# A branch turned round: the soft experts' stage as the fall-through arm

## The chip, the cores and the metric

One core of a Trainium2 chip. The metric is the device time of one execution in microseconds (us); the median of three runs of the kernel before is 814.7 us.

## The reference

Attention whose queries are averaged in pairs, then a layer that sends each of 2304 tokens to one of 8 experts, then a layer of 32 soft slots (4 for each of 8 experts). All arrays are float32.

```python
attn = softmax(scale * mean_of_2(q) @ k.T) @ v       # 4 x 8 heads, 1152 keys, 64 wide
x = attn.reshape(2304, 512)
e = argmax(x @ w_gate + bias); x = gate * relu(x @ w1[e]) @ w2[e]
logits = x @ phi                                     # 2304 x 32
slot_in  = softmax(logits, over tokens).T @ x        # 32 x 512
slot_out = relu(slot_in @ m2w1[e]) @ m2w2[e]         # 4 slots for each e
out = softmax(logits, over slots) @ slot_out         # 2304 x 512
```

## The kernel before

It has three stages: attention (to about 520 us), the experts (`ffn`, to about 760 us), the soft experts (`soft_moe`, to the end). All is written out in order by hand (`manual_schedule`): each engine works through its instructions in the order in which the program text issues them, and the framework adds semaphore waits.

The experts work on tasks of 256 tokens of one expert. The routing decides at run time how many there are. Eight (`NSTAT`) are written out; `g["n"]` holds the real count, which every engine reads into a register (L1660). Only if it is over 8 does `more` (L1662) run a loop of further tasks, the rare tasks: `with tc.If(g["n"] > NSTAT)` at L1666, with no other arm. With these inputs it is not over 8, so each engine's branch at L1666 jumps past the rare tasks' instructions. The rare block borrows the last four weight tiles as working room and loads them again at its end (L1669, four transfers by SP). A single matmul on the first weight tile (`NBR`, L1316) stands just ahead of the branch.

While tasks run, `Front.group` folds finished tokens into running sums: logits (L872, L876), a running maximum, `acc`, and the logits' transposed copy `lT`, which GpSimd scatters to DRAM (L918). The last group also makes the slot inputs `siT` (L850, L851).

`soft_moe` reads 32 weight tiles of 1 MB (`Stream`): 22 are fetched while the experts run, 10 as tiles come free. Its loop is paced by `step()` (L1455), once for each weight tile taken: it fetches, does what is in `todo`, and two entries of the list `soft` from the twelfth step on. At the first step SP loads all logits as `L` (L1459). `soft` normalises `L` over the slots and then, for each of five groups q of up to four token blocks, does two things. `c4(q)` is one copy on VectorE (L1386) of four blocks of `L` into `Cr`, a tile of which there is one (`CRB = 1`). `cT(q)` is four transposes of `Cr` on TensorE (L1392), a copy of the result to `cs` on ScalarE (L1394) and two subtractions on VectorE (L1396). Both halves of the expert layer are TensorE work on the weight tiles (L1472, L1486). The output is made in column parts (L1439), copied to `ob` (L1441) and stored by SP (L1443). `so` shares the place of `Cr`.

Of the kernel before, what the change touches and what calls it, by code (L numbers as in the profile page):

```python
# [24 lines left out]
DM = H * D  # L25
# [40 lines left out]
NWB = 0  # L66
NWR = (1, 1, 4)
RAWS = (1, 3)
CRB = 1
NBR = 1  # L70
WARM = 0
FILL = (0, 0, 2, 0, 0, 0, 2, 2, 2, 2)
# [720 lines left out]
class Front:  # L793
# [61 lines left out]
    def group(self, last=False):  # L855

        nc, g, xp = self.tc.nc, self.g, self.xp
        V = nc.vector
        bs, self.blocks = self.blocks, []
        n4 = len(bs)  # L860
        m = n4 * 32
        lanes = lambda c: slice(c * 32, (c + 1) * 32)
        small = lambda name: xp.tile([128, 128], F32, name=name, bufs=1)
        bank = lambda name: g["ps"].tile([128, 512], F32, name=name, tag="mx", bufs=3)
        d = {}

        def logits():
            lt = bank("lt")[:, 0:128]
            for c in range(n4):
                h, row = bs[c]["h"], bs[c]["row"]  # L870
                hot = g["ident"][:, row:row + 1] if isinstance(row, int) else row
                nc.tensor.matmul(lt[lanes(c)], hot.to_broadcast([128, NSL]), g["neg"][:, h * 128:(h + 1) * 128],  # L872
                                 start=True, stop=False)
            for k in range(4):
                for c in range(n4):
                    nc.tensor.matmul(lt[lanes(c)], g["phis"][:, k], bs[c]["yT"][:, k], start=False, stop=(k == 3))  # L876
            d["ls"], d["ex"] = small("ls"), small("ex")
            d["al"], d["se"], new = (xp.tile([128, 1], F32, name=x, bufs=2) for x in ("al", "se", "new"))
            d["al"], d["se"], nm = d["al"][:m], d["se"][:m], new[:m]
            V.reduce_max(d["se"], lt[:m], axis=AX.X)  # L880
            V.tensor_scalar(out=nm, in0=d["se"], scalar1=-1.0, scalar2=g["nm"][:m], op0=ALU.mult, op1=ALU.min)
            nc.scalar.activation(d["ex"][:m], lt[:m], AF.Exp, bias=nm)
            d["lt"] = lt
            nc.scalar.activation(d["al"], g["nm"][:m], AF.Exp, bias=nm, scale=-1.0)
            if m < 128:
                V.tensor_copy(g["nm"][:m], nm)
            else:
                g["nm"] = new

        def keep():  # L890
            V.tensor_copy(d["ls"][:m], d["lt"][:m])

        def flip():
            ep = bank("ep")
            d["eT"] = small("eT")
            nc.tensor.transpose(ep[:, :m], d["ex"][:m], g["ident"][:m, :m])
            nc.scalar.copy(d["eT"][:, :m], ep[:, :m])

        def turn_logits():
            lp = bank("lp")  # L900
            d["lT"] = g["lT"]
            nc.tensor.transpose(lp[:, :m], d["ls"][:m], g["ident"][:m, :m])
            V.tensor_copy(d["lT"][:, :m], lp[:, :m])

        def add():
            V.reduce_sum(d["se"], d["ex"][:m], axis=AX.X)
            V.scalar_tensor_tensor(out=g["sums"][:m], in0=g["sums"][:m], scalar=d["al"], in1=d["se"], op0=ALU.mult, op1=ALU.add)

        def rows():
            sin = bank("sin")  # L910
            for c in range(n4):
                nc.tensor.matmul(sin[lanes(c)], d["eT"][:, lanes(c)], bs[c]["y"], start=True, stop=True)
            V.scalar_tensor_tensor(out=g["acc"][:m], in0=g["acc"][:m], scalar=d["al"], in1=sin[:m], op0=ALU.mult, op1=ALU.add)

        def store(cs):
            done = []
            for c in cs:
                wr = nc.gpsimd.indirect_dma_start(out=g["ls"], out_offset=bass.IndirectOffsetOnAxis(ap=bs[c]["idx"], axis=0),  # L918
                                                  in_=d["lT"][:, lanes(c)], in_offset=None)
                for w in done:  # L920
                    self.tc.declare_no_dep(wr.ins, w.ins, reason="the rows are distinct")
                done.append(wr)
                if c != cs[-1]:
                    nc.gpsimd.memset(g["nop"], 0.0)


        twice = [c for c in range(n4) if bs[c]["row"] is AROW]
        rest = [c for c in range(n4) if c not in twice]
        first, late = (lambda: store(twice or rest)), (lambda: store(rest) if twice else None)
        if not last:  # L930
            return [None, logits, keep, None, flip, turn_logits, add, first, None, rows, None, late]
        common, weights, spread, total, slots = self.combine()
        return [None, logits, None, common, keep, None, flip, None, turn_logits, None, weights, None, add, spread, first, rows, None, total, None, slots]


# [103 lines left out]
def ffn(ctx, tc, g):  # L1039
# [214 lines left out]
    open_more(NWR[len(RAWS)])  # L1254
    flush(FILL)

    def more(room):

        own = room[1][:, 1024:2048]
        tio, pio, cnt = own[:, 0:MAXT], own[:, 16:17], own[:, 17:18]  # L1260
# [1 line left out]
            nc.gpsimd.iota(o, pattern=pat, base=0, channel_multiplier=cm, allow_small_or_imprecise_dtypes=True)  # L1262
        nc.gpsimd.memset(cnt, float(NSTAT))
        with tc.For_i(NSTAT, g["n"], 1):
            task(room, own, tio, pio, cnt)

    def task(room, own, tio, pio, cnt):

        V = nc.vector
        hot, on, tmp = own[:, 18:19], own[:, 32:32 + MAXT], own[:, 64:64 + 4 * MAXT].rearrange("p (q t) -> p q t", q=4)  # L1270
# [36 lines left out]
                nc.tensor.matmul(yp[h], ht[:, f, h * 128:(h + 1) * 128], wr[f // 2 % 2][:, c:c + DM], start=(f == 0), stop=(f == KF - 1))  # L1307
        todo.extend(front.put(yp, s["gt"], [xidx[:, h:h + 1] for h in range(2)], hot))
        todo.extend(front.group(True))
        flush()  # L1310


    warm = ps.tile([128, 512], F32, name="warm", tag="mx", bufs=3)
    first = g["ws"].tiles["m2w1", 0][0]
    for _ in range(NBR):
        nc.tensor.matmul(warm, g["ones128"], first[:, 0:512], start=True, stop=True)  # L1316
    g["more"](more)


class Stream:  # L1320


    def __init__(self, tc, g):
        self.tc, self.g = tc, g
        self.keys = [(w, i) for w in ("m2w1", "m2w2") for i in range(16)]
        self.tiles = {}
        self.free = []
        self.next = 0

    def add(self, pool, n):  # L1330
        self.free += [pool] * n

    def fetch(self, eng=None):
        if self.next < len(self.keys) and self.free:
            key = self.keys[self.next]
            pool = self.free.pop(0)
            tl = pool.tile([128, 2048], F32, name="mw")
            (eng or self.tc.nc.sync).dma_start(out=tl, in_=self.g[key[0]][key[1]])
            self.tiles[key] = (tl, pool)
            self.next += 1  # L1340
            return True
        return False

    def take(self, *key):
        tl, pool = self.tiles.pop(key)
        self.free.append(pool)
        return tl


def warm_up(nc, g, o, n):  # L1350
# [4 lines left out]
def soft_moe(ctx, tc, g):  # L1355
# [4 lines left out]
    V = nc.vector  # L1360
    cp = ctx.enter_context(tc.tile_pool(name="s_cp", bufs=1))
    siT = g["siT"]
    L = cp.tile([128, NI, NSL], F32, name="L")
    T3 = [128, NI, NSL]
    NR = (NI + 3) // 4
    if NWB:
# [15 lines left out]

    def c4(q):
        n4 = min(4, NI - 4 * q)
        Cr[q] = cp.tile([128, 4, 4, NSL], F32, name="Cr", tag="Cr", bufs=CRB)
        V.tensor_copy(Cr[q][:, :n4], L[:, 4 * q:4 * q + n4].unsqueeze(2).to_broadcast([128, n4, 4, NSL]))  # L1386

    def cT(q):
# [18 lines left out]
        lambda: c4(0),  # L1407
    ]
    for q in range(NR):
        if q + 1 < NR:  # L1410
            soft.append(lambda q=q: c4(q + 1))
        soft.append(lambda q=q: cT(q))

    def relu(r, hp):
        hs = cp.tile([128, 2, 512], F32, name="hs")
# [11 lines left out]
    def out_steps(h):  # L1427
# [5 lines left out]

        def some(i, c, i0, n4, ob):
            if i == i0:
                ob[0] = g["wa"].tile([128, 2048 // dw, dw], F32, name="ob", tag="mw")
            fo = bank("hp", 4).rearrange("p (c d) -> p c d", c=n)
            for k in range(c):
                nc.tensor.matmul(fo[:, k], cs[:, i + k], SO[h], start=True, stop=True)  # L1439
# [34 lines left out]
        todo += relu(r, hp)  # L1474
    first = [2 * KF * d0 // 512 for d0, _ in PARTS]
    for h, (d0, dw) in enumerate(PARTS):
        so = cp.tile([128, 2, DM // 2], F32, name="so", tag="Cr", bufs=CRB)[:, :, :dw]
        na = 512 // dw
        for r in range(2):
            op = bank("op", 2)[:, 0:dw]  # L1480
# [32 lines left out]
def moe_kernel(tc, qT, kT, vT, wg, mod, mbias, w1, w2, phi, m2w1, m2w2, k0, q0, out):  # L1513
    nc = tc.nc
    with ExitStack() as ctx:
# [2 lines left out]
        gf = c4.enter_context(tc.tile_pool(name="gf", bufs=1))  # L1518
        ga = c3.enter_context(tc.tile_pool(name="ga", bufs=1, side="right"))
        keep = {**dict.fromkeys(("ident", "ones128", "si", "sel", "xidx", "axidx", "nop"), gp),  # L1520
                **dict.fromkeys(("widx", "xidx", "ntask", "C", "agt", "awidx", "neg", "acc", "sums", "nm", "lT", "m4", "nmc", "w", "siw", "rc"), gf)}
        dr = ctx.enter_context(tc.tile_pool(name="dr", bufs=1, space=DRAM))
        g = dict(qT=qT, kT=kT, vT=vT, wg=wg, w1=w1, w2=w2, phi=phi, m2w1=m2w1, m2w2=m2w2, k0=k0, q0=q0, out=out)
        g["xs"] = dr.tile([PAD + N, XW], F32, name="xs")
# [21 lines left out]
        T([TB, NTB, 4], "sm")  # L1546
        T([TB, NTB, E], "ex")
        T([128, NSL], "si")
        g["phis"] = gf.tile([128, DM // 128, NSL], F32, name="phis")
        T([128, N // TS + 1], "jts")  # L1550
        T([128, MAXT], "tio")
        T([128, E], "eio")
# [3 lines left out]
            T([128, 1], nm)  # L1556
        T([128, NSL], "i32")
        T([1, 1], "nop")
        T([128, TS], "neg")
        T([128, DM], "acc")  # L1560
        T([128, 1], "sums")
        T([128, 1], "nm")
        T([128, 128], "lT")
        T([1, 4, NSL], "m4")
        T([128, 1], "nmc")
        T([128, 1], "w")
# [92 lines left out]
        def load_count():  # L1659
            g["n"] = nc.values_load(g["ntask"][0:1, 0:1], min_val=N // TS - 1, max_val=MAXT)  # L1660

        def more(task):  # L1662
            keys = list(ws.tiles)[-4:]
            room = [ws.tiles[key][0] for key in keys]

            with tc.If(g["n"] > NSTAT):  # L1666
                task(room)
                for key, tl in zip(keys, room):
                    nc.sync.dma_start(out=tl, in_=g[key[0]][key[1]])  # L1669

        g["load_count"] = load_count
        g["more"] = more
        with tc.manual_schedule():
            make_identity(nc, ident)
            g["ws"] = ws = Stream(tc, g)
# [1 line left out]
            with ExitStack() as c2:  # L1677
# [13 lines left out]
                g["open"] = open_weights  # L1691
                with ExitStack() as c1:
                    ffn(c1, tc, g)
            c4.close()
            with ExitStack() as c1:
                soft_moe(c1, tc, g)


def _layout(inputs):
# [41 lines left out]
```

## Time and profile before

| what | value |
|---|---|
| median of three runs | 814.7 us (814.34 to 814.75) |
| the profiled execution | 816.65 us |
| its span in the trace | 814.9 us |
| TensorE, VectorE, ScalarE, GpSimd busy | 96%, 69%, 57%, 66% |
| TensorE's instructions | 5674 matmuls, 5674 weight loads |
| granted TensorE clock, mean | 0.996 |

PE is TensorE's matmuls, PEld its weight loads, DVE VectorE, ACT ScalarE, POOL GpSimd, SP SyncE. A q behind a name (PEldq, SPq) is the engine's instruction queue: branches, semaphore events, DMA issues. "issue" is time in which an engine waited for nothing that the profile shows.

### The profile page before, as it was taken

What the parts mean: (1) busy time and instruction counts of PE and PEld (TensorE: products, weight loads), DVE (VectorE), ACT (ScalarE), POOL (GpSimd) and SP (SyncE); (2) the same over time, 40 slices, a digit from 0 to 9 for tenths busy, and PEclk for the clock granted to TensorE, in tenths of its full rate; (3) what the DMA queues carried; (4) which work ended last, traced back from release to release, by engine and by line L of the source; (5) the groups of instructions that cost most, each with busy time, mean ns of one, the idle gap of its engine ahead of it and who ended that gap; (6) DMA issues with size and microseconds to landing.
All of it is one profiled execution on the core that took longest, in us unless ns stands there. A gap on an engine that the chain in (4) does not pass through costs nothing.

```text
span 814.9 us, 15864 instructions
## 1 busy us (share of the span) xinstructions
PE 782.9 (96%) x5674; PEld 595.9 (73%) x5674; DVE 565.8 (69%) x1171; ACT 461.2 (57%) x1096; POOL 541.8 (66%) x501
## 2 busy tenths in 40 slices
PE   5899999999999999999999999999999999999897
PEld 5677777766677776777666668788898689988356
DVE  7587777678777877877878785766666556664252
ACT  5456565666865658766556873455555545554133
POOL 6879899999888988879978963534635544450200
PEclk9999999999999999999999999999999999999999
DMA  9876558667655676755554120786787887767987
GB/s 323 232 208 157 156 146 221 158 172 178 148 158 149 149 199 168 176 136 151 127 141 140 52 80 12 223 291 237 274 279 264 261 287 260 272 208 260 341 364 233
DMA packets 57782, 162.80 MB, mean 200 GB/s; under 512 B 14443, under 2 KB 21915, under 8 KB 53595
## 3 DMA queue, kind: packets, MB, share of 16 engines
q1 hardware_dynamic: 41604, 98.05, 42.7%
q0 software_dynamic: 13648, 47.32, 17.4%
q10 hardware_dynamic: 2448, 16.39, 5.6%
q8 instruction: 46, 0.75, 0.4%
q14 instruction: 36, 0.29, 0.1%
HBM read 110.45 MB, written 10.89 MB: 149 GB/s over the span
## 4 chain that ended last, share of the span: by engine, by line
PE 82%; DVE 5%; ACT 4%; POOL 3%; issue 3%; DMA 2%; SPq 0%; ACTq 0%; POOLq 0%; DVEq 0%
PE pv L272 17%; PE sc L252 12%; PE sc L258 8%; PE mps L203 7%; PE hp L774 4%; PE hp L776 4%; PE hp L775 4%; PE yp L788 4%; PE yp L790 3%; PE yp L789 3%; PE sg L305 2%; PE hp L1472 2%; PE op L1486 2%; PE tp L332 2%; DVE mxp L205 1%
## 5 line engine op out<-in xcount | busy, mean ns | idle before, releaser
L285 POOL TENSOR_TENSOR acc<-acc,e 128x576 f32<-128x576 f32 x214 | 315.2, 1473 | 23.6 <-ACT e L262 10.1
L262 ACT ACTIVATE e<-sc 128x288 f32<-128x288 f32 x576 | 223.7, 410 | 138.8 <-PE sc L258 116.1
L205 DVE TENSOR_REDUCE mxp<-mps 128x1 f32<-128x384 f32 x432 | 220.5, 549 | 94.2 <-PE mps L203 86.4
L252 PE MATMUL sc<-QS,KS 128*128 128x288 f32 x576 | 186.0, 331 | 3.3 <-ACT e L262 3.1
L258 PE MATMUL sc<-QL,KH 69*128 69x288 f32 x576 | 170.0, 298 | 1.5 <-DVE QL L223 1.2
L272 PE MATMUL pv<-e,V 128*64 128x288 f32 x1152 | 161.8, 416 | 0.0
L252 PEld LDWEIGHTS sc<-QS,KS 128*128 128x128 f32 x576 | 109.2, 190 | 56.4 <-issue 27.1
L203 PE MATMUL mps<-KS,QS 128*128 128x384 f32 x384 | 134.9, 356 | 11.5 <-ACT QS L468 7.0
L744 POOL DMA_INDIRECT wraw<-in_w,widx x72 | 73.9, 1026 | 106.3 <-DVE wlo L766 82.7
L272 PEld LDWEIGHTS pv<-e,V 128*64 128x64 f32 x1152 | 74.4, 137 | 60.2 <-issue 22.2
L258 PEld LDWEIGHTS sc<-QL,KH 69*128 69x128 f32 x576 | 109.3, 190 | 2.0 <-DVE QL L223 1.4
L766 DVE TENSOR_TENSOR wlo<-wraw,whi 128x512 fp32r<-128x512 f32 x136 | 90.7, 689 | 27.1 <-ACT whi L765 22.8
L765 ACT CAST whi<-wraw 128x512 fp32r<-128x512 f32 x136 | 79.6, 619 | 18.2 <-DMA wraw<-in_w,widx 14.0
L203 PEld LDWEIGHTS mps<-KS,QS 128*128 128x128 f32 x384 | 74.4, 194 | 14.8 <-ACT QS L468 7.4
L774 PE MATMUL hp<-xh,whi 128*128 128x256 f32 x256 | 73.2, 286 | 0.0
L776 PE MATMUL hp<-xh,wlo 128*128 128x256 f32 x256 | 71.9, 281 | 1.0 <-issue 0.8
L775 PE MATMUL hp<-xl,whi 128*128 128x256 f32 x256 | 71.8, 280 | 0.3 <-DVE xl L761 0.3
L283 POOL TENSOR_TENSOR acc<-e 128x576 f32<-128x576 f32 x31 | 44.7, 1441 | 35.8 <-ACT e L262 35.7
L781 ACT ACTIVATE hh<-hp 128x256 fp32r<-128x256 f32 x64 | 24.5, 384 | 72.8 <-PE hp L776 55.6
L782 DVE SCALAR_TENSOR_TENSOR hl<-hp,hh 128x256 fp32r<-128x256 f32 x64 | 27.1, 424 | 42.7 <-ACT hh L781 39.6
L788 PE MATMUL yp<-whi,hh 128*128 128x512 f32 x128 | 53.0, 414 | 0.7 <-ACT hh L781 0.6
L774 PEld LDWEIGHTS hp<-xh,whi 128*128 128x128 f32 x256 | 48.1, 188 | 4.8 <-ACT whi L765 1.3
(397 smaller groups left out, 1233.2 us busy)
## 6 DMA issues: line engine op xcount, KB each, us to landing
mw<-in_m2w SPq DMA_DIRECT2D x17, 1024.0 KB, 6.8
mw<-in_m2w ACTq DMA_DIRECT2D x15, 1024.0 KB, 7.2
V<-in_vT SPq DMA_DIRECT2D x16, 576.0 KB, 3.6
KX<-in_kT SPq DMA_DIRECT2D x15, 576.0 KB, 4.0
QX<-in_qT SPq DMA_DIRECT2D x15, 576.0 KB, 5.9
KS<-KC SPq DMA_DIRECT2D x30, 288.0 KB, 5.3
KH<-KC SPq DMA_DIRECT2D x30, 288.0 KB, 4.6
QS<-QC SPq DMA_DIRECT2D x60, 144.0 KB, 3.9
```

Source lines behind the costliest of these rows:

```text
L203: nc.tensor.matmul(mps[:, :384], s["QS"][:, j, blk * 128:(blk + 1) * 128], s["KS"][:, j, ks], start=True, stop=True)
L205: V.reduce_max(s["mxp"][:, slot, t:t + 1], mps[:, :384], axis=AX.X)
L252: nc.tensor.matmul(sc[:, :NU], s["KS"][:, j, c * 128:(c + 1) * 128], s["QS"][:, j, u * NU:(u + 1) * NU], start=True, stop=False)
L258: nc.tensor.matmul(sc[:, :NU], s["KH"][0:69, j, c * 128:(c + 1) * 128], s["QL"][0:69, j, u * NU:(u + 1) * NU], start=False, stop=True)
L262: nc.scalar.activation(s["e", u, c][:, j], sc[:, :NU], AF.Exp, scale=SM)
L272: nc.tensor.matmul(pv[j * 64:(j + 1) * 64, :NU], s["v"][:, j, c, :], e[:, j], start=(c == 0), stop=(c == NKB - 1))
L285: eng.tensor_add(s["acc", u], s["acc", u], s["e", u, c])
L766: nc.vector.tensor_sub(lo, x, hi.bitcast(F32))
L774: nc.tensor.matmul(hp, wh[:, c], xh[:, k], start=(k == 0), stop=False)
L775: nc.tensor.matmul(hp, wh[:, c], xl[:, k], start=False, stop=False)
L776: nc.tensor.matmul(hp, wl[:, c], xh[:, k], start=False, stop=(k == DM // 128 - 1))
L788: nc.tensor.matmul(yp[h], hh[:, hs], wh, start=(f == 0), stop=False)
```

## The change

- The branch gets two arms. The first, for a count of 8 or less, holds the whole soft experts' stage; it stands right behind the branch. The other holds the rare tasks (`rare`, formerly `more` and `task` in `ffn`), then `ws.again()`, which starts the stream of 32 weight tiles over, and a second copy of `soft_moe`.
- What both arms read must outlive the experts' stage: the pool `gf` is closed behind the arms; the last group's maximum gets a tile of its own, `lastnm`.
- `L` is no longer a tile of the soft stage: it is the new tile `both`, whose parts are also `neg`, `phis` and `lT`. `Cr` and `so` are views of `acc`.
- In `soft`, `cT(q)` now stands ahead of `c4(q + 1)`; it stood behind it.
- The weight stream holds fixed tiles instead of pool slots; the output tiles `ob` come from it (`spare`).

```diff
@@ Front.group, logits
+            if last and m == 128:
+                new = g["lastnm"]
@@ ffn, its end
-    warm = ps.tile([128, 512], F32, name="warm", tag="mx", bufs=3)
-    first = g["ws"].tiles["m2w1", 0][0]
-    for _ in range(NBR):
-        nc.tensor.matmul(warm, g["ones128"], first[:, 0:512], start=True, stop=True)
-    g["more"](more)
+    warm = ps.tile([128, 512], F32, name="warm", tag="mx", bufs=3)
+    first = g["ws"].tiles["m2w1", 0]
+    for _ in range(NBR):
+        nc.tensor.matmul(warm, g["ones128"], first[:, 0:512], start=True, stop=True)
@@ Stream
+        new = [pool.tile([128, 2048], F32, name="mw") for _ in range(n)]
+        self.all += new
+        self.free += new
+    def again(self):
+        self.tiles, self.free, self.next = {}, list(self.all), 0
+    def spare(self):
+        assert self.next == len(self.keys)
+        return self.free.pop(0)
@@ soft_moe
-    L = cp.tile([128, NI, NSL], F32, name="L")
+    L = g["both"].rearrange("p (i s) -> p i s", s=NSL)
-        Cr[q] = cp.tile([128, 4, 4, NSL], F32, name="Cr", tag="Cr", bufs=CRB)
+        Cr[q] = g["acc"].rearrange("p (c a s) -> p c a s", c=4, a=4)
     for q in range(NR):
+        soft.append(lambda q=q: cT(q))
         if q + 1 < NR:
             soft.append(lambda q=q: c4(q + 1))
-        soft.append(lambda q=q: cT(q))
-                ob[0] = g["wa"].tile([128, 2048 // dw, dw], F32, name="ob", tag="mw")
+                ob[0] = ws.spare().rearrange("p (c d) -> p c d", d=dw)
-        so = cp.tile([128, 2, DM // 2], F32, name="so", tag="Cr", bufs=CRB)[:, :, :dw]
+        so = g["acc"].rearrange("p (r d) -> p r d", r=2)[:, :, :dw]
@@ moe_kernel
-            with tc.If(g["n"] > NSTAT):
-                task(room)
-                for key, tl in zip(keys, room):
-                    nc.sync.dma_start(out=tl, in_=g[key[0]][key[1]])
+            with tc.If(g["n"] <= NSTAT) as arm:
+                with ExitStack() as c1:
+                    soft_moe(c1, tc, g)
+            with arm.Else():
+                with ExitStack() as c1:
+                    rare(c1, tc, g)
+                ws.again()
+                with ExitStack() as c1:
+                    soft_moe(c1, tc, g)
             c4.close()
-            with ExitStack() as c1:
-                soft_moe(c1, tc, g)
```

## Rows read from the trace of the kernel before

**Rows 1.** The page: the last chain's shares by engine; one instruction-loading queue (packets, MB).

```profile
PE 82%; DVE 5%; ACT 4%; POOL 3%; issue 3%; DMA 2%; SPq 0%; ACTq 0%; POOLq 0%; DVEq 0%
...
q8 instruction: 46, 0.75, 0.4%
```

**Rows 2.** The chain of waits around the branch: start us, us, what.

```profile
760.00 0.50 issue
760.50 2.78 PE hp L1472 x22
763.27 1.38 issue
764.65 6.17 PE hp L1472 x50
```

**Rows 3.** The branch's line: engine, operation, count, duration ns min/median/max, first and last start.

```profile
L1666 SPq EVENT_SEMAPHORE  x4: 17/17/17, 752.6 to 752.9; - x4
...
L1666 PEldq COMPARE_BRANCH  x1: 445/445/445, 758.1 to 758.1; - x1
...
L1666 DVEq COMPARE_BRANCH  x1: 72/72/72, 759.8 to 759.8; - x1
...
L1666 DVEq EVENT_SEMAPHORE  x1: 21/21/21, 760.3 to 760.3; - x1
```

**Rows 4.** VectorE's timeline at the branch: start us, us, instruction, idle before it.

```profile
759.75 0.29 DVE L851 TENSOR_TENSOR siT<-sp,rc 128x128 f32<-128x128 f32 x1 [1.44 <-PE sp L850]
```

**Rows 5.** Instruction-loading queues in 756 to 762 us, then in 762 to 764 us.

```profile
q14 instruction: 2, 0.02, 0.7%
...
q8 instruction: 1, 0.02, 3.4%
```

**Rows 6.** The timeline of 777 to 787 us, all engines.

```profile
777.92 0.66 PE L1392 MATMUL tp<-ident,Cr 128*128 128x128 f32 x4
...
778.61 0.59 ACT L1394 CAST cs<-tp 128x512 fp32r<-128x512 f32 x1 [3.72 <-PE tp L1392]
778.61 0.43 DVE L1386 COPY Cr<-L 128x512 f32<-128x512 f32 x1 [1.17 <-PE tp L1392]
...
779.23 1.39 DVE L1396 TENSOR_TENSOR cs<-tp,cs 32x512 fp32r<-32x512 f32 x2 [0.19 <-ACT cs L1394]
...
781.24 0.60 PE L1392 MATMUL tp<-ident,Cr 128*128 128x128 f32 x4
...
782.77 0.66 PE L1392 MATMUL tp<-ident,Cr 128*128 128x128 f32 x4
...
784.62 0.63 PE L1392 MATMUL tp<-ident,Cr 128*128 128x128 f32 x4 [0.19 <-DVE Cr L1386]
...
785.93 0.29 DVE L1386 COPY Cr<-L 128x256 f32<-128x256 f32 x1
...
786.37 0.41 PE L1392 MATMUL tp<-ident,Cr 128*128 128x128 f32 x2
```

**Rows 7.** Busy time by stretch: us, PE, PEld, DVE, ACT, POOL, PEclk, DMA share, GB/s.

```profile
781.20:786.70 5.50, 5.19 (x64) 2.70 (x62) 5.05 (x9) 1.76 (x3) 0.00 (x0) 1.00 1.02 420
...
795.00:809.30 14.30, 14.29 (x256) 12.47 (x255) 5.02 (x10) 5.81 (x15) 0.00 (x0) 1.00 0.82 258
```

**Rows 8.** The tail: ScalarE's last copy; SP's semaphore events at the end; at L1459.

```profile
809.38 0.58 ACT L1441 COPY ob<-hp 128x512 f32<-128x512 f32 x1 [0.31 <-PE hp L1439]
...
L1737 SPq EVENT_SEMAPHORE  x14: 17/28/28, 810.4 to 814.9; - x14
...
L1459 SPq EVENT_SEMAPHORE  x7: 17/28/28, 765.4 to 765.7; - x7
```

**Rows 9.** TensorE's clock: a gap, the stretch behind it, and the stretch behind the branch.

```profile
32.45 0.41 PE L203 MATMUL mps<-KS,QS 128*128 128x384 f32 x1 [2.73 <-DMA KS<-KL]
...
33.90:37.30 3.40, 3.40 (x16) 2.11 (x13) 0.42 (x2) 0.65 (x2) 0.53 (x2) 0.50 1.00 376
...
760.00:764.65 4.65, 2.78 (x23) 0.81 (x23) 0.04 (x1) 0.00 (x0) 0.96 (x1) 1.00 0.86 287
```

More of the change, by code (lines that the diff above doesn't have):

```diff
@@ L68 @@
 RAWS = (1, 3)
-CRB = 1
 NBR = 1
@@ L1255, in ffn, with rare, more @@
     flush(FILL)
-    def more(room):
+    warm = ps.tile([128, 512], F32, name="warm", tag="mx", bufs=3)
+    first = g["ws"].tiles["m2w1", 0]
+    for _ in range(NBR):
+        nc.tensor.matmul(warm, g["ones128"], first[:, 0:512], start=True, stop=True)
+def rare(ctx, tc, g):
+    nc = tc.nc
+    KD, KF = DM // 128, F // 128
+    xp = ctx.enter_context(tc.tile_pool(name="r_xp", bufs=2))
+    ps = g["ps"] = ctx.enter_context(tc.tile_pool(name="r_ps", bufs=2, space=PSUM))
+    room = g["ws"].all[-4:]
+    front = Front(tc, g, xp)
+    todo = []
+    def more():
         own = room[1][:, 1024:2048]
@@ L1264, in more, with task @@
         with tc.For_i(NSTAT, g["n"], 1):
-            task(room, own, tio, pio, cnt)
-    def task(room, own, tio, pio, cnt):
+            task(own, tio, pio, cnt)
+    def task(own, tio, pio, cnt):
         V = nc.vector
@@ L1309, in task @@
         todo.extend(front.group(True))
-        flush()
-    warm = ps.tile([128, 512], F32, name="warm", tag="mx", bufs=3)
-    first = g["ws"].tiles["m2w1", 0][0]
-    for _ in range(NBR):
-        nc.tensor.matmul(warm, g["ones128"], first[:, 0:512], start=True, stop=True)
-    g["more"](more)
+        while todo:
+            f = todo.pop(0)
+            if f:
+                f()
+    more()
 class Stream:
@@ L1326, in __init__ @@
         self.tiles = {}
-        self.free = []
+        self.all, self.free = [], []
         self.next = 0
     def add(self, pool, n):
-        self.free += [pool] * n
+        new = [pool.tile([128, 2048], F32, name="mw") for _ in range(n)]
[3 more added lines that the diff above has]
+        self.tiles, self.free, self.next = {}, list(self.all), 0
     def fetch(self, eng=None):
@@ L1335, in fetch @@
             key = self.keys[self.next]
-            pool = self.free.pop(0)
-            tl = pool.tile([128, 2048], F32, name="mw")
+            tl = self.tiles[key] = self.free.pop(0)
             (eng or self.tc.nc.sync).dma_start(out=tl, in_=self.g[key[0]][key[1]])
-            self.tiles[key] = (tl, pool)
             self.next += 1
@@ L1344, in take @@
     def take(self, *key):
-        tl, pool = self.tiles.pop(key)
-        self.free.append(pool)
-        return tl
+        tl = self.tiles.pop(key)
+        self.free.append(tl)
+        return tl
+    def spare(self):
+        assert self.next == len(self.keys)
+        return self.free.pop(0)
 def warm_up(nc, g, o, n):
@@ L1520, in moe_kernel @@
         keep = {**dict.fromkeys(("ident", "ones128", "si", "sel", "xidx", "axidx", "nop"), gp),
-                **dict.fromkeys(("widx", "xidx", "ntask", "C", "agt", "awidx", "neg", "acc", "sums", "nm", "lT", "m4", "nmc", "w", "siw", "rc"), gf)}
+                **dict.fromkeys(("widx", "xidx", "ntask", "C", "agt", "awidx", "acc", "sums", "nm", "lastnm", "m4", "nmc", "w", "siw", "rc"), gf)}
         dr = ctx.enter_context(tc.tile_pool(name="dr", bufs=1, space=DRAM))
@@ L1548, in moe_kernel @@
         T([128, NSL], "si")
-        g["phis"] = gf.tile([128, DM // 128, NSL], F32, name="phis")
+        both = g["both"] = gf.tile([128, NI * NSL], F32, name="both")
+        g["neg"] = both[:, 0:TS]
+        g["phis"] = both[:, TS:TS + 128].rearrange("p (k s) -> p k s", s=NSL)
+        g["lT"] = both[:, TS + 128:TS + 256]
         T([128, N // TS + 1], "jts")
@@ L1558, in moe_kernel @@
         T([1, 1], "nop")
-        T([128, TS], "neg")
         T([128, DM], "acc")
@@ L1562, in moe_kernel @@
         T([128, 1], "nm")
-        T([128, 128], "lT")
+        T([128, 1], "lastnm")
         T([1, 4, NSL], "m4")
@@ L1660, in load_count @@
             g["n"] = nc.values_load(g["ntask"][0:1, 0:1], min_val=N // TS - 1, max_val=MAXT)
-        def more(task):
-            keys = list(ws.tiles)[-4:]
-            room = [ws.tiles[key][0] for key in keys]
-            with tc.If(g["n"] > NSTAT):
-                task(room)
-                for key, tl in zip(keys, room):
-                    nc.sync.dma_start(out=tl, in_=g[key[0]][key[1]])
         g["load_count"] = load_count
-        g["more"] = more
         with tc.manual_schedule():
```

## Prediction

> **What bounds the kernel now.** I read the page first, then the chain that ended last, then, for the soft experts' stage alone, the timeline and the busy time by stretch. The chain lies on TensorE for 82% of the span, and waits named "issue" make 3% [rows 1]. The soft stage is no exception: between 781.2 and 786.7 us TensorE is busy 5.19 of 5.50 us, between 795 and 809.3 us 14.29 of 14.30 us [rows 7]. So what delays or frees TensorE anywhere from 760 us on moves the end by as much, unless an idle stretch behind it takes it up, and there are almost none. The last transfers follow the last copy: ScalarE ends it at 809.96 us and the span ends at 814.9 us [rows 8]; that tail of 4.9 us moves with TensorE too. Two places matter more than the rest: the branch at 758 to 765 us, where TensorE idles 0.50 and 1.38 us [rows 2], and the five groups of `c4` and `cT` at 777 to 787 us.
>
> **The branch, start of the stage.** The 0.50 us ahead of the first matmul of L1472: `siT`, its operand, ends at 759.75 + 0.29 = 760.04 us [rows 4]. VectorE takes its branch at 759.8 and only at 760.3 runs the semaphore event behind it [rows 3]; TensorE starts at 760.50, just after. With the stage as the fall-through arm, no event that evens out the arms' counts stands there, and the matmul waits for `siT` itself. The hand-over from VectorE to TensorE is 786.37 - (785.93 + 0.29) = 0.15 us in [rows 6], so the start is at 760.15 to 760.2: a gain of 0.35 us (bounds 0 and 0.46). The 1.38 us: it begins after 22 matmuls of the stage and has no releaser [rows 2]. TensorE's instruction loads are the q8 packets: 46 for 11,348 instructions, 247 each [rows 1]. None lies in 756 to 762 us, and one does in 762 to 764 us, in the idle time itself [rows 5]. I read that as follows: the jump landed near the end of instructions already on the core, and the next packet had not been asked for in time. Straight-line code shows no such gap in the rows of this stage, so I take the whole 1.38 us as gained (bounds 0 and 1.38). Both together: 0.35 + 1.38 = 1.73, say 1.7 us.
>
> [...]
>
> Nothing else of the start is on the path. SP's load of `L` need not wait for events at the merge any more and comes earlier, but its first reader stands behind work of TensorE and VectorE. The weight tiles are fetched in the same order into the same number of tiles; with the transfers at a share of 1.02, TensorE was busy 5.19 of 5.50 us and waited for no tile [rows 7], so fixed tiles cost nothing. If that cover were gone, a late tile would hold TensorE until it has landed; I count 0. `lastnm` and `spare` change names and add no instruction.
>
> **The order of `cT` and `c4`.** This is the large term. Two `soft` entries run per weight tile, in both kernels, and TensorE's order is the same. VectorE's is not. Before, it copied `Cr` for group q + 1 as soon as TensorE had read group q (778.61, ahead of the two subtractions of 779.23 [rows 6]), so the transposes of the next group found their operand ready. Now the two subtractions of group q stand ahead of that copy on VectorE, and they wait for ScalarE's copy of the transposed group. From one group's transposes to the next the chain is now serial; from [rows 6]:
> - transposes to the start of ScalarE's copy: 778.61 - 777.92 = 0.69
> - ScalarE's copy 0.59, and 0.03 to VectorE (779.23 - 779.20)
> - the two subtractions 1.39
> - the copy `c4` 0.43 (0.29 for the last group, of two blocks)
> - to TensorE 0.15
>
> That is 3.28 us, and 3.14 us to the last group. For group 1 nothing is lost: its operand would be ready at 779.23 + 1.39 + 0.43 + 0.15 = 781.20, and its transposes stood at 781.24 anyway, behind the transposes of the other work. For groups 2, 3 and 4 the starts were 782.77, 784.62 and 786.37, which is 5.13 us from group 1 to group 4; the new distance is 3.28 + 3.28 + 3.14 = 9.70 us. TensorE executes in order, and the next weight tile's matmuls stand behind the waiting transposes, so the difference is idle time: 9.70 - 5.13 = 4.57, say 4.5 us. Who is queued behind: L1486's 16 matmuls of each tile, and by them all the rest. The bounds are 0 (if VectorE's copies still come in time) and 4.9 (with a hand-over of 0.15 at each of the steps). I take 4.5, since every step has its duration in a row.
>
> **The end of the first arm.** The jump is not removed but moved: behind the last store each engine must get past the other arm. At the branch of before, SP ran four events with counts [rows 3], as many as the rare block has SP transfers of its own. The other arm now issues 32 weight loads against 10, so SP has such events at the end of the first arm, each after the transfers that it counts, the last stores among them. Only then come the end's waits. In the trace of before these start at 810.4 us, while the last stores are still on their way, so they cost nothing [rows 8]. Fourteen events stand there; seven in a row took 765.4 to 765.7, 0.05 us each [rows 8], so some twelve behind the last landing are 0.6 us. The events of the arm's end and the branch add about 0.3 us: four took 752.6 to 752.9 [rows 3]. Together 0.9 us. Bounds: 0, if nothing waits behind the landing, and 6.5 us, which is TensorE's branch at 758.1 [rows 3] to its return at 764.65 [rows 2], the dearest jump that this trace holds. I take 0.9, near the short end, because SP's jump of before was short; TensorE's new jump is long (over 320 pairs of instructions in the two stretches of [rows 7] alone), but it can run while the stores land.
>
> **Sum.** - 1.7 + 4.5 + 0.9 = + 3.7 us. On the profiled execution that is a span of 814.9 + 3.7 = 818.6 and a time of 816.65 + 3.7 = 820.35; that execution lies 1.95 above the median of the runs, so for the median I forecast 814.7 + 3.7 = 818.4 us.
>
> **Rivals.**
> 1. The copies are in time after all. Place: `c4` on VectorE at 781 to 787. Price: the 4.5 us. It decides as soon as the distance between two groups' transposes stays under the 1.9 us of before. Against it: `Cr` is one buffer in both kernels, and VectorE followed the text's order in the trace of before. For it: I know the order from the text only. Then - 1.7 + 0.9: 813.9 us, not slower.
> 2. The same, and a tail that costs nothing because the events come before the last landing: 814.7 - 1.7 = 813.0 us.
> 3. TensorE's clock falls. With some 1.6 us of work in each 3.28 us it is half idle for 10 us. [...] Against it: the stretch 760 to 764.65, busy 2.78 of 4.65 us with a gap of 1.38, stayed at 1.00 [rows 9]. 3.4 us at half speed lose 1.7: 820.1 us. [...]
> 4. SP's jump at the end waits for its instructions, behind the last landing where nothing hides it. The price lies between VectorE's 0.4 us (759.87 to 760.3) and 6.5 us; about the middle, 3 us on top: 821.4 us.
> 5. The change doesn't do what it says: the first arm is not laid behind the branch, or the 1.38 us has another cause and stays. Then the 1.7 us are not gained: 820.1 us.
>
> **How the numbers follow.** Forecast 0.38 (its own range 817.3 to 819.5: the gain between 1.4 and 1.8, the stall between 4.0 and 4.9, the tail between 0.6 and 1.4); rival 1 0.20; rival 2 0.13; rival 3 0.10; rival 4 0.12; rival 5 0.07. About 0.2% (1.6 us) can be told from no change, so faster is under 813.1 and slower over 816.3. Rival 2 is faster, 0.13; rival 1 is the same, 0.20; the rest are slower, 0.67. The range runs from rival 2 to rival 4, 813.0 to 821.4; half of each of these two lies outside, 0.13 in all.
>
> **What would show it.** Right: no idle of over a microsecond on TensorE in its first 10 us of the stage; the first matmul of L1472's code within 0.2 us of `siT`; transposes of `Cr` 3.1 to 3.3 us apart from group 1 on, with "<-DVE Cr" as their releaser and 1.4 to 1.6 us of idle each; VectorE's copies of `Cr` behind the subtractions; SP's end waits behind the last landing. Wrong: transposes under 2 us apart (rival 1), a clock of 0.50 near 785 us (rival 3), over 6.5 us from ScalarE's last copy to the end of the span (rival 4), a gap like the old one at the start (rival 5).

## The result and the profile after

The changed kernel takes 819.5 us (median of six runs, 817.9 to 821.1), the kernel before 814.7 us (six runs, 814.2 to 816.4): a ratio of 1.0056, interval 1.0041 to 1.0072, or 3.3 to 5.9 us more. The forecast was 818.4 us. The profiled execution took 819.08 us, its span is 817.4 us; the mean granted clock is 0.996 in both. In the new file L1472 has become L1494, L1486 L1508, L1392 L1414, L1386 L1408, L1439 to L1443 L1461 to L1465, and the branch stands at L1708.

The chain of waits around the branch after (start us, us, what):

```profile
758.70 0.12 issue
758.83 7.93 PE hp L1494 x72
```

The 72 matmuls run in one piece, in 7.93 us. Before, the same 72 went from 760.50 to 764.65 + 6.17 = 770.82 us, 10.32 us [rows 2]: 2.39 us more, although the idle time shown is 1.38 us. The rest lies in the order of the matmuls, as TensorE's weight loads in the kernel before show:

```profile
762.21 0.15 PEld L1472 LDWEIGHTS hp<-mw,siT 128*32 128x32 f32 x3 [0.27 <-issue]
764.65 0.15 PEld L1472 LDWEIGHTS hp<-mw,siT 128*32 128x32 f32 x7 [2.29 <-issue]
...
769.37 0.11 PEld L1472 LDWEIGHTS hp<-mw,siT 128*32 128x32 f32 x1 [0.27 <-issue]
769.80 0.11 PEld L1472 LDWEIGHTS hp<-mw,siT 128*32 128x32 f32 x1 [0.32 <-issue]
```

These matmuls fill 32 columns each (128*32) and run four side by side: the four of a group start within 0.05 us of one another, and in the kernel after a group starts every 0.43 us, 18 groups in all. Before, two groups ahead of the gap are a matmul short, and two matmuls come alone at the end, 0.43 us each. So the gap cost some 1.6 us of pace (the seventh group starts at 764.65 and not at 763.07 us) and the two lone matmuls some 0.9 us. A single matmul is as long in both kernels, 589 to 617 ns.

The timeline after, around `cT` and `c4` (answers to [rows 6]):

```profile
777.17 0.62 PE L1414 MATMUL tp<-ident,acc 128*128 128x128 f32 x4
...
777.83 0.59 ACT L1416 CAST cs<-tp 128x512 fp32r<-128x512 f32 x1 [0.86 <-PE tp L1414]
778.45 1.40 DVE L1418 TENSOR_TENSOR cs<-tp,cs 32x512 fp32r<-32x512 f32 x2 [0.38 <-ACT cs L1416]
779.88 0.43 DVE L1408 COPY acc<-both 128x512 f32<-128x512 f32 x1
...
780.45 0.63 PE L1414 MATMUL tp<-ident,acc 128*128 128x128 f32 x4 [1.65 <-DVE acc L1408]
...
783.73 0.63 PE L1414 MATMUL tp<-ident,acc 128*128 128x128 f32 x4 [1.65 <-DVE acc L1408]
...
786.44 0.30 DVE L1408 COPY acc<-both 128x256 f32<-128x256 f32 x1
...
786.88 0.41 PE L1414 MATMUL tp<-ident,acc 128*128 128x128 f32 x2 [1.52 <-DVE acc L1408]
```

The copy stands behind the subtractions, and the transposes are 3.28, 3.28 and 3.15 us apart: 9.71 us from group 1 to group 4 against 5.13 us, 4.58 us more. The busy time by stretch (columns as in [rows 7]) shows the idle TensorE: 2.50 us busy where it was 5.19.

```profile
781.20:786.70 5.50, 2.50 (x36) 1.10 (x28) 3.45 (x6) 1.08 (x2) 0.00 (x0) 1.00 1.01 419
```

The granted clock stayed at 1.00. Behind the last group the chain of waits after has a piece that nobody forecast:

```profile
788.92 3.37 PE op L1508 x69
792.29 0.24 issue
792.53 0.49 PE op L1508 x9
```

From the last group's transposes to ScalarE's last copy it is now 810.52 - 786.88 = 23.64 us; before it was 809.38 - 786.37 = 23.01 [rows 6, 8]. This costs 0.63 us. The same 80 matmuls (69 + 11) took 3.60 us in one piece before. The DMA queues in 786 to 789.9 and in 789.9 to 790.4 us (packets, MB, share):

```profile
q1 hardware_dynamic: 216, 1.64, 101.1%
...
q8 instruction: 1, 0.02, 13.3%
```

In the first 3.9 us the weights fill the transfers and no instruction load comes; one starts at 790.12 us, as they end, and TensorE goes on at 792.53, 1.35 us behind that packet's end. That full transfers as such hold a load back is not shown: in the kernel before one came in the middle of them, at 784.18 us, and TensorE lost nothing (queues in 784 to 785 us):

```profile
q1 hardware_dynamic: 62, 0.41, 99.0%
q8 instruction: 1, 0.02, 6.6%
```

The tail after: ScalarE's last copy, SP's stores (count, ns min/median/max) and their time to landing, SP's last steps, and the branch's line:

```profile
810.52 0.59 ACT L1463 COPY mw<-hp 128x512 f32<-128x512 f32 x1 [0.31 <-PE hp L1461]
...
L1465 SPq DMA_DIRECT2D out<-mw x9: 372/392/1687, 796.4 to 812.2; - x9
...
DMA to landing us min/median/max: 3.7/3.8/3.9
...
L1758 SPq DRAIN  x3: 7/7/13, 816.5 to 816.8; - x3
...
L1708 SPq COMPARE_BRANCH  x2: 37/45/53, 751.1 to 812.7; - x2
...
L1708 PEldq COMPARE_BRANCH  x2: 95/2039/3983, 756.8 to 809.2; - x2
```

The kernel before, same views:

```profile
L1443 SPq DMA_DIRECT2D out<-ob x9: 372/373/457, 795.3 to 810.0; - x9
...
DMA to landing us min/median/max: 1.8/2.3/2.8
...
L1737 SPq DRAIN  x3: 7/7/7, 814.0 to 814.4; - x3
```

From the copy's end to the span's end it is 6.3 us against 4.9 [rows 8], 1.3 us more (a page gives spans to 0.1 us; unrounded they are 817.37 and 814.94 us). It isn't spent behind the landing: from SP's first drain to the end both take 0.9 us. The last store was issued 1.1 us behind the copy's end instead of at once, because an issue on SP took 1.69 us; the other 0.2 us is the last store's own landing.

From the stage's first matmul to the end: 814.9 - 760.50 = 54.40 us before, 817.4 - 758.83 = 58.57 us after. The parts make up the difference: - 2.39 + 4.58 + 0.63 + 1.3 = + 4.1 us (unrounded, 4.10). The stage starts 1.67 us earlier, 0.31 of it by the change (0.15 us behind `siT` instead of 0.46); the rest arises ahead of the changed code, and such starts lay between 755.96 and 762.61 us over the executions below. So the change's parts make + 3.8 us, inside the interval of 3.3 to 5.9; the medians' + 4.8 us is 1.0 more, which no part accounts for.

### The profile page after: what moved, and what is told of

Read it like the earlier page. It is cut to its first block, busy times and chain, and to the rows that moved or that the text cites. A ratio compares the mean times of both kernels' runs of the same rounds, so it can differ in the third digit from the quotient of the medians.

```text
span 817.4 us, 15854 instructions
## 1 busy us (share of the span) xinstructions
PE 781.7 (96%) x5674; PEld 594.8 (73%) x5674; DVE 566.8 (69%) x1171; ACT 461.9 (57%) x1096; POOL 543.6 (67%) x501
## 4 chain that ended last, share of the span: by engine, by line
PE 85%; DVE 5%; ACT 4%; DMA 2%; issue 2%; POOL 1%; SPq 0%; ACTq 0%; POOLq 0%; DVEq 0%
PE pv L271 17%; PE sc L251 12%; PE sc L257 8%; PE mps L202 7%; PE hp L773 4%; PE hp L775 4%; PE hp L774 4%; PE yp L787 4%; PE yp L789 4%; PE yp L788 4%; PE sg L304 2%; PE hp L1494 2%; PE tp L331 2%; PE op L1508 1%; DVE mxp L204 1%
```

## The experiments

The theory: the gap behind the branch, the order, the last transposes' stall and the tail are separate sums, the gap, the stall and the tail all coming from where TensorE's instruction loads fall. What ties a wait to a load is the packets of the traces: the executions below have the gap twice, the stall twice and seven jumps of over 3 us on TensorE, and each of these eleven times TensorE goes on 1.3 to 1.5 us behind the end of a load's packet (764.65 behind 763.16 us before, 792.53 behind 791.18 after). The rival for the gap and the tail: other edits of the change (fixed tiles, the borrowed places) cause them. The stage's time, from its first matmul to the end, is the measure that the executions' differing starts don't touch. It is of one execution each, good to 0.05 us, and leaves out what a jump costs ahead of it; the change of a median departs from that of the stage by up to 1.5 us:

| kernel | ratio to before (interval) | median, before's, us | stage, us |
|---|---|---|---|
| before | | | 54.40 |
| after | 1.0056 (1.0041 to 1.0072) | 819.5, 814.7 | 58.57 |
| order back | 0.9995 (0.9982 to 1.0009) | 813.9, 814.2 | 54.23 |
| order alone | 1.0057 (1.0040 to 1.0073) | 818.8, 814.2 | 58.88 |
| short jump | 1.0030 (1.0016 to 1.0043) | 817.1, 814.2 | 58.05 |
| before, 40 matmuls | 0.9991 (0.9975 to 1.0007) | 813.8, 814.2 | 52.08 |
| before, 52 matmuls | 0.9992 (0.9977 to 1.0007) | 813.9, 814.3 | 52.09 |
| no branch | 1.0029 (1.0018 to 1.0041) | 816.1, 814.3 | 56.64 |
| no branch, order back | 0.9966 (0.9955 to 0.9978) | 811.8, 814.3 | 52.13 |
| order back, 44 matmuls | 1.0009 (0.9993 to 1.0025) | 815.2, 814.3 | 54.19 |
| order back, 20 matmuls | 1.0003 (0.9992 to 1.0014) | 814.5, 814.3 | 53.19 |
| order back, 30 matmuls | 0.9994 (0.9984 to 1.0004) | 813.9, 814.3 | 53.07 |

**The order, taken back.** The kernel after, with a second place for `Cr` so that the copy can go ahead again:

```diff
-    Cr = {}
+    Cr, odd = {}, []
...
+        if q == 1:
+            odd.append(ws.spare()[:, 0:512])
-        Cr[q] = g["acc"].rearrange("p (c a s) -> p c a s", c=4, a=4)
+        Cr[q] = (odd[0] if q % 2 else g["acc"]).rearrange("p (c a s) -> p c a s", c=4, a=4)
...
-        soft.append(lambda q=q: cT(q))
         if q + 1 < NR:
             soft.append(lambda q=q: c4(q + 1))
+        soft.append(lambda q=q: cT(q))
```

> The changed kernel with a second place for Cr (a free weight tile for the odd groups) and the copies ahead of the subtractions again. If the order on VectorE costs 4.5 us: 819.5 - 4.5 = 815.0 us, transposes of Cr 1.5 to 1.9 us apart. If the late transposes were hidden behind the transfers and the loss sits elsewhere: 819.5 us. The gain at the start and the longer tail stay as they are in both.

```profile
776.62 0.60 PE L1416 MATMUL tp<-ident,mw 128*128 128x128 f32 x4
...
781.75 0.41 PE L1416 MATMUL tp<-ident,acc 128*128 128x128 f32 x2
...
787.84 0.62 PE L1510 MATMUL op<-mw,hT 128*32 128x128 f32 x10 [0.61 <-issue]
```

This timeline has 5.13 us from group 1 to group 4, as before: the 4.58 us are gone. The stall behind the last group is larger, though (0.61 us of idle shown, 1.1 us in all), and the tail stays long (6.1 us): the two eat the 2.39 us of the branch, and the time equals that of before. The median of 813.9 us is 1.1 under the expectation.

**The order alone**, in the kernel before:

```diff
+        soft.append(lambda q=q: cT(q))
         if q + 1 < NR:
             soft.append(lambda q=q: c4(q + 1))
-        soft.append(lambda q=q: cT(q))
```

> The kernel before with cT(q) ahead of c4(q + 1) and nothing else: VectorE's order alone is changed. If that order costs TensorE 4.5 us: 814.7 + 4.5 = 819.2 us, transposes 3.28 us apart, the stall of the branch stays. If something else of the change made the transposes late (acc, L in another place): 814.7 us.

The timeline has the same 9.71 us, with no other part of the change:

```profile
778.14 0.62 PE L1392 MATMUL tp<-ident,Cr 128*128 128x128 f32 x4
...
787.85 0.41 PE L1392 MATMUL tp<-ident,Cr 128*128 128x128 f32 x2 [1.52 <-DVE Cr L1386]
```

The median rose by 4.6 us, the distance by 4.58. The order is shown both ways, and a third time by the two kernels without a branch below (56.64 and 52.13 us, 4.51 apart).

**The short jump.** The kernel after, its other arm without the second copy of the stage:

```diff
             with arm.Else():
                 with ExitStack() as c1:
                     rare(c1, tc, g)
-                ws.again()
-                with ExitStack() as c1:
-                    soft_moe(c1, tc, g)
```

> The changed kernel whose other arm holds the rare tasks alone, without the second copy of the soft stage (left out; it does not run with these inputs). The first arm's jump at the end is then some 330 TensorE instructions long and not some 1,600. If the 6.3 us from the last copy to the end (4.9 before) come from the load of TensorE's far instructions in between the stores: 4.9 to 5.3 us and 819.5 - 1.2 = 818.3 us. If the late last store is chance or belongs to the arms as such: 6.3 us and 819.5 us.

The branch's line and SP's stores:

```profile
L1708 PEldq COMPARE_BRANCH  x2: 95/248/402, 754.7 to 806.4; - x2
...
L1465 SPq DMA_DIRECT2D out<-mw x9: 372/387/2043, 793.6 to 809.8; - x9
```

TensorE's branch at the end takes 402 ns instead of 3983, and the tail is as long as ever, 6.4 us. So the wait in the jump is not what the tail costs. The median of 817.1 us lies under both expectations, in part because the stall behind the last group is gone: the same 80 matmuls run in one piece (chain).

```profile
786.77 3.60 PE op L1508 x80
```

Nothing ahead of that place was changed. The load that came 31.3 us behind the stage's first matmul in the kernel after came 28.3 us behind it here, with the transfers still full. So the stall can go without any shift of code.

**No branch at all.** The kernel after with the first arm's body alone:

```diff
-            with tc.If(g["n"] <= NSTAT) as arm:
-                with ExitStack() as c1:
-                    soft_moe(c1, tc, g)
-            with arm.Else():
-                ...
+            with ExitStack() as c1:
+                soft_moe(c1, tc, g)
```

> The changed kernel without branch, rare tasks and second copy (left out; they do not run with these inputs): the soft stage stands straight behind the experts. If the late last store comes from the load of TensorE's instructions behind the jump at the arm's end, beside the stores: 4.9 to 5.2 us from the last copy to the end, as in the kernel before, and 819.5 - 1.2 = 818.3 us or a little less. If it comes from the other edits (ob in other tiles, for one): 6.1 to 6.4 us stay, and 819.5 us. The order on VectorE stays as changed, 3.28 us apart.

```profile
755.96 7.93 PE hp L1494 x72
...
L1465 SPq DMA_DIRECT2D out<-mw x9: 372/373/457, 792.9 to 807.6; - x9
```

The median of 816.1 us is lower than expected (818.3 or a little less). The chain keeps the 7.93 us, and SP's issues take 457 ns at most, as before the change; the tail is 5.0 us. The output tiles come from `spare` here too, so the tiles are not the tail's cause. What is left is the order: 54.40 - 2.39 + 4.58 = 56.6 us, and 56.64 was measured.

**No branch, the old order**: both edits together.

> The same without branch, with the old order and two places for Cr. If the terms add up: the kernel before less the 2.8 us of its branch, 814.2 - 2.8 = 811.4 us, up to 812.5 if a load of instructions holds TensorE once behind the last transposes, as it did for 0.6 and 1.1 us in two of the arms' runs. If the tail is not the jump's: 1.2 us more, 812.6 to 813.7.

```profile
758.07 7.93 PE hp L1496 x72
```

A stage of 52.13 us, 54.40 - 2.39 = 52.0; the median is 2.5 us under that of before. It is the only kernel here that is faster than both by more than the measurement's uncertainty. It cannot take over from them: it has no code for a count over 8.

**Where the loads end, in the kernel before.** Small matmuls on a zero tile at the front were to shift all later code against the ends of the 16 KB loads (0.75 MB in 46 packets [rows 1]; from the load at 35.49 us to the one at 731.78, 38 loads on, TensorE starts some 250 instructions to a load). Each is four instructions of TensorE, two matmuls and two weight loads, as the one of L1316 is in the trace:

```diff
+        z = sp.tile([128, 32], F32, name="z", bufs=1)
+        V.memset(z, 0.0)
+        for _ in range(40):
+            nc.tensor.matmul(wp[0:32, 0:32], z, z, start=True, stop=True)
         warm(SWARM[0])
         khi(0, 0)
```

> The kernel before with 40 small matmuls on zeros, 160 TensorE instructions, in the idle time ahead of the first attention matmul; they move every later TensorE instruction by 160 places. If the stall of 2.4 us behind the branch comes from where in a load of some 256 instructions the jump lands (47 before its end), it lands with some 200 left less the shift's rest, about 140, and the stall is gone: 814.7 - 2.4 = 812.3 us. If any jump over the rare tasks costs that much: 814.7 us, with the gap still there.

The chain and the branch's line:

```profile
759.22 7.93 PE hp L1476 x72
...
L1670 PEldq COMPARE_BRANCH  x1: 3185/3185/3185, 755.7 to 755.7; - x1
```

Nothing of the branch was changed, and the gap of 2.39 us is gone; so it is a matter of place. In exchange the jump itself waits, 3185 ns on TensorE against 445 [rows 3]: the first matmul starts 2.24 us behind `siT` (756.98 us), not 0.46. Net - 0.6 us, too little to tell in the medians. With 52 matmuls both waits were to vanish:

> The kernel before with 52 small matmuls (208 TensorE instructions) ahead of its first matmul; 40 took the stall behind the branch away but left the jump waiting for its target, 1.8 us, because the load boundary lay right at the branch. If place within a load decides both: some 48 instructions between boundary and jump and some 95 behind it, so both waits are gone or under 0.5 us, and 814.2 - 2.2 = 812.0 us. If a jump costs 2 us wherever it lies: 813.8 us as with 40.

They did not: the branch took 3065 ns, the rest as with 40. This expectation was wrong, and the count of places by which it was made is not to be trusted. What stands is that the gap came in both executions without extra matmuls (the kernel before and the order alone, 10.32 and 10.21 us for the 72) and in neither with them.

**Where the loads end, with the order back.** The same matmuls in the first experiment's kernel (on a part of `acc`), 44, 20 and 30 of them:

> The changed kernel with the old order and two places for Cr, and 44 small matmuls (176 TensorE instructions) ahead of its first matmul. If the 1.1 us behind the last transposes came from a load that waits behind the weight transfers, the boundary now lies about 80 instructions earlier in the weights' stretch with the next one behind it, so TensorE takes 22.7 us from the last transposes to its last matmul (23.8 without the shift): 813.9 - 1.1 = 812.8 us. If the wait has nothing to do with the place: 23.8 us and 813.9 us. The tail of 6.1 us stays in both.

> e1 with 20 matmuls on a zero tile (40 instructions... each of the 20 compiles to 4, so 80 of TensorE) at the front, which move the ends of the 16 KB instruction loads against the code. If the waits behind the last transposes (1.1 us in e1) and the overlap of two loads with the last stores (tail 7.0 us with 44 matmuls against 6.1 without) both follow from where a load ends: a load is asked ahead of the weights' last burst as with 44, and only the jump's own load falls beside the last stores as without. Then no stall of over 0.3 us between 781 and 800 us, 6.0 to 6.4 us from ScalarE's last copy to the end, 53.1 us from the stage's first matmul to the end (before 54.4), ratio about 0.998. If place does not decide: stall 1.1, tail 6.1 to 7.0, 54.2 us or more, ratio 0.9995 to 1.001.

> The same with 30 matmuls (120 instructions): by place, the same as with 20, 53.1 us from the stage's first matmul to the end and a ratio of about 0.998; if place does not decide, 54.2 us or more.

The line of SP's stores with 44, the chain with 20, and with 30:

```profile
L1471 SPq DMA_DIRECT2D out<-mw x9: 372/394/2385, 792.2 to 808.7; - x9
```

```profile
762.61 7.93 PE hp L1500 x72
```

```profile
758.13 7.93 PE hp L1500 x72
```

All three lost the stall of 1.1 us. That this is due to place is not shown: the short jump lost the stall too, without any shift, and each is one execution. With 44 the tail rose to 7.0 us, as two loads fell beside the last stores (packets at 805.5 and 806.0 us), which the expectation had not counted, and the median is 815.2 us where 812.8 was expected; with 20 and 30 it was 6.0. The stage took 53.19 and 53.07 us where 53.1 was expected. The medians did not follow: ratios of 1.0003 and 0.9994, where 0.998 was expected. With 20, the stage began at 762.61 us, later than in any other execution; by the author's estimate the shift moves the loads of the 750 us ahead as well, but whether these give the gain back was not settled.

## Why the prediction was right

The direction and the mechanism of the large term held. That the sum held as well is in part luck: the branch gave 1.0 us more than forecast, and the tail and a stall that was not forecast took 1.0 us more. The median, 819.5 us, lies at the upper end of the forecast's own 817.3 to 819.5.

- **The order of `cT` and `c4`: right.** + 4.5 us forecast, 4.58 us measured in the changed kernel, and both single experiments give it. Steps and releaser are as forecast; the idle time is 1.65, 1.65 and 1.52 us where 1.4 to 1.6 was named. Rivals 1 and 2 are out.
- **The branch: the cause right, the size too small.** Forecast - 1.7 us, of it 0.35 for the hand-over (measured 0.31) and 1.38 for the gap. The gap was worth 2.39 us: the step that failed is reading its price off the chain's "issue". The stall also broke up the groups of four that run side by side, and two matmuls ran alone at the end; the sound measure is the time of the same 72 matmuls with and without it. The hand-over's mechanism holds only in part: the first matmul starts 0.12 us behind the single matmul ahead of it on TensorE, which ends at 758.70 us, when `siT` is ready too (758.68); in seven of the later kernels `siT` was ready 0.66 to 0.72 us ahead of it, so there the matmul did not wait for `siT`. Rival 5 is out: the first arm stands behind the branch and the gap is gone, as it is without a branch.
- **The end of the first arm: nearly the right size (0.9 forecast, 1.3 measured), the wrong mechanism; that the sizes are near is luck.** The forecast put events of SP at the arm's end, behind the last landing. SP has none on the branch's line; its branch ends at 812.7 us, and the last landing is at 816.3. Instead the last stores are issued late and land late. In the packets of the trace, 15 of the 16 pieces of one store had ended by 811.06 us and the last at 812.87; a TensorE instruction load of 1.55 us stands beside them at 810.09. No jump at the end, no extra tail: without the branch it is 5.0 us, in the other five kernels that jump there 6.0 to 7.0. In all six the long issue on SP ends 0.40 to 0.44 us behind the end of such a load's packet (812.05 behind 811.63 us after), also in the short jump, where TensorE waited 402 ns. That the load holds the late piece up is the author's estimate from these times; no run separates the load from the jump itself, so this last link is not shown by an experiment.
- **Rival 4** is out: SP's jump took 53 ns at most. The long jump is TensorE's (3983 ns), and it runs while the stores land, as the forecast had allowed. **Rival 3**, whose price is the 3.40 us at 0.50 in [rows 9], is out: the clock stayed at 1.00 through three half-idle stretches (TensorE busy 0.99 of 2.60 us from 777.8 us on, 0.88 of 2.50 from 781.2, 0.96 of 2.40 from 784.4).
- **Missing: the stall behind the last group, 0.63 us.** The forecast counted TensorE's instruction loads only at the jumps. Here, on straight-line code, a load came late, and TensorE stood until 1.35 us behind its end. Why it came late is open: it started as the weights' transfers ended, but with the order back a load that came in the middle of them, at 785.35 us, left the larger stall.

## What to carry to other kernels

When two pieces of work share one buffer and one engine that follows the text's order, write the copy that frees the next group ahead of the work that waits for another engine; here two swapped lines cost 4.6 us, more than all that the branch could give. Price a stall by the time of the same instructions without it, not by the idle time that the trace names. Moving a jump did not remove its price here: in the kernels above it was 2.4 us behind the landing, 1.7 to 1.8 us in the jump, or 1.0 to 2.1 us beside the last stores.

## What was not expected of the hardware

- TensorE stalled on straight-line code behind a late instruction load: 0.6 us in the kernel after, 1.1 us with the order back. Full transfers don't settle it, since loads at 784.18 us before and 784.95 us in the short jump came amid them and cost nothing. The runs with 80, 120 or 176 more instructions at the front have no such stall, but neither has the short jump, whose code ahead of the place is that of the kernel after.
- One taken jump of unchanged length on TensorE took 445, 3185 or 3065 ns, by 0, 160 or 208 instructions put in front of the whole program; where it was cheap, the loss came 22 matmuls behind its landing. The two long waits ended 1.4 and 1.5 us behind the end of a load's packet.
- The stall among matmuls that run side by side cost more than its idle time: 1.38 us were shown idle and 2.39 us lost, 0.9 of it because two matmuls then ran alone.
